# Moving the seventh product of a seven-product matrix multiply into the phase that makes its operands

## The chip, the cores and the metric

The kernel runs on one NeuronCore of a Trainium2 chip. The metric is the device time of one execution in microseconds (us). TensorE is called PE here, VectorE DVE, ScalarE ACT, GpSimd POOL, and SyncE, which only issues DMAs in this kernel, SP.

## The reference

Two stages are chained. The first is an attention between 512 tokens and 32 state vectors for 8 batches and 8 heads of width 64, in both directions. The second is a feed-forward layer on its 8 x (512 + 32) = 4352 output rows of width 512.

```python
scores = 0.125 * x @ state^T;  xread = softmax(scores) @ state        # 512 rows per batch
scores2 = 0.125 * state @ x^T; sread = softmax(scores2) @ x           # 32 rows per batch
y = concat([xread, sread], rows)                                      # [4352, 512]
h = y @ w_in;  g = h * sigmoid(h);  out = g @ w_out                   # 512 -> 2048 -> 512
```

The max that the reference takes off before each exp is left out by the kernel; the softmax is the same without it.

## The kernel before, in words

Everything is issued in an order written out by hand; no scheduler reorders it. Each engine, and each DMA queue, works through its own list in that order and stops at an instruction whose inputs or buffers aren't ready.

For one batch the hidden layer is made transposed, in 16 tiles of 128 hidden units by 512 tokens. One such tile is a "G1 step" (`emit_G1`): two matmuls with 512 columns each on the normalised attention weights `aT` and on `W1` (the state times `w_in`, made by small matmuls `ps_w1` and copied to SBUF in "pieces" of 512 columns, one half by DVE and the other by ACT), and one ACT instruction that applies silu and writes `g`. `upto(k)` issues all G1 steps up to number k. The tiles of `h` go through two PSUM banks (`h1`), used in turn.

The output product g @ w_out (G2) is done for the first batch, number 0, and for the 256 gathered sread rows, numbered as batch 8, with plain matmuls. For batches b = 1 to 7 class `Unit` does it by Strassen's scheme in Winograd's form: tokens are halved (columns 0:256 and 256:512 of `g`), hidden units are halved (`lo` = tiles 0 to 7, `hi` = tiles 8 to 15), output columns are halved, and seven half-size products take the place of eight. Product p has 8 "unit steps" (`u.mm(p, k)`), each two matmuls with 256 columns. Right sides are the quarters of `w_out` (B11 to B22) and their sums D1 to D4 (`wt`). Left sides are quarters of `g` and sums `s1`, `s2` and others that DVE forms (`sums12`, `sums3`, `sums4`). Products 2, 3 and 4 go to a PSUM bank `be`, the others are added up in a bank `al`; the two banks are tags `o0` and `o1` and change places from batch to batch. In between, copies of `al` are taken (`snap`), and the four blocks of the output tile pair `o[0]`, `o[1]` (`block(i, c)`) are put together by adds on DVE and POOL. `out_half(i)` stores one tile.

One batch b runs like this on PE. (1) The G1 phase: the remaining G1 steps of the batch (6 are already done for b > 1), with 13 unit steps of products 1 and 2 strewn in (`early`). (2) The rest of product 2, and "group A" (`group_a`): `ps_w1` pieces, transposed scores of a later batch, and for some batches the `ps_sr` matmuls. For b = 1 scores of batch 2 come before product 6, and group A after it. (3) Products 6, 4, 5. (4) "Group B": up to three more `ps_w1` pieces, for b = 1, 2, 3, 4 and 6; where there are three, the third goes through the `h1` banks. (5) Products 3 and 7 with the first six G1 steps of the next batch (or steps of batch 8 at b = 7) between them. What is left of a batch, the last copy, add and store (`finish_last`), is issued in the next batch's G1 phase.

Beside this run: the x tiles of later batches, fetched by SP DMAs (`fetch_x`), cast by POOL (`cast_x`, four casts), transposed by SP DMA transposes (`transpose_x`); the attention's normalisation (`norm`, `norm_t`; the latter's multiplication is shared by POOL and DVE) and the DMA transpose of its result to `aT`; copies of x rows (`spread_x`), of states (`evict_state`), and the rest of the weight sums (`t_weights`) on DVE in the first G1 phases. ACT changes its function table to exp and back to silu once per batch up to b = 5: after product 2 for `exps_t`, and back after the `snap` that follows product 6; the copies of group A's `W1` pieces stand behind that.

Of the kernel before, what the change touches and what calls it, by code (L numbers as in the profile page):

```python
# [8 lines left out]
FP32 = mybir.dt.float32  # L9
# [9 lines left out]
B = 8  # L19
# [6 lines left out]
NFT = DF // 128  # L26
# [16 lines left out]
def kernel(  # L43
# [8 lines left out]
    nc = tc.nc  # L52
    ds = bass.ds
# [104 lines left out]
    def copy(eng, dst, src):  # L158
        if eng is nc.scalar:
            nc.scalar.activation(dst, src, func=COPY, bias=0.0)  # L160
        else:
            eng.tensor_copy(dst, src)  # L162
# [407 lines left out]
    def G2(b, tt, ft):  # L570
        if ft == 0:
            if b == 0 and tt >= 2:
                outs[tt] = psA.tile([128, DM], FP32, tag=f"a{tt - 2}", name="o_a")
            else:
                i = tt % 2
                outs[tt] = psO.tile([128, DM], FP32, tag=f"o{i}", name="o")
        nc.tensor.matmul(  # L577
            outs[tt][:],
            gt[b * NFT + ft][:, ds(128 * tt, 128)],
            w_out_sb[:, ft, :],  # L580
            start=(ft == 0),
            stop=(ft == NFT - 1),
            skip_group_check=True,
        )
# [5 lines left out]
    def sub(eng, dst, a, c):  # L590
        eng.tensor_tensor(dst, a, c, op=SUB)  # L591

    def add(eng, dst, a, c):
        eng.tensor_tensor(dst, a, c, op=ADD)  # L594
# [13 lines left out]
    class Unit:  # L608
        def __init__(self, b):
            self.b = b  # L610
            self.lo, self.hi = gh[b, 0], None
            self.s1 = spool.tile([128, 8, 256], BF16, tag="s1", name="s1")
            self.s2 = spool.tile([128, 8, 256], BF16, tag="s2", name="s2")
            self.al = psO.tile([128, 2, 256], FP32, tag=f"o{b % 2}", name="o")
            self.be = None
            self.o = [
                opool.tile([128, 2, DM], FP32, tag=f"o_sb{i}", name="o_sb") for i in range(2)
            ]

        def snap(self, eng):  # L620
            t = spool.tile([128, 2, 256], FP32, tag=f"snap{len(self.kept) % 2}", name="snap")
            self.kept.append(t)
            copy(eng, t[:], self.al[:])

        kept = None

        def mm(self, p, k):
            hi, lo = self.hi, self.lo
            left, right = {
                1: (lambda: lo[:, k, 0:256], B11),  # L630
                2: (lambda: hi[:, k, 0:256], B21),
                3: (lambda: hi[:, k, 0:256], B22),
                4: (lambda: hi[:, k, 256:512], D4),
                5: (lambda: self.s1[:, k], D1),
                6: (lambda: self.s2[:, k], D2),
                7: (lambda: lo[:, k, 256:512], D3),
            }[p]
            left = left()
            if p in (2, 3, 4):
                if k == 0:  # L640
                    self.be = psO.tile(
                        [128, 2, 256], FP32, tag=f"o{1 - self.b % 2}", name="o"
                    )
                to, first = self.be, k == 0
            else:
                to, first = self.al, p == 1 and k == 0
            for t in range(2):
                nc.tensor.matmul(  # L648
                    to[:, t, :],
                    left[:, ds(128 * t, 128)],  # L650
                    right[:, k, :],
                    start=first and t == 0,
                    stop=(k == 7),
                    skip_group_check=True,
                )
# [11 lines left out]
        def sums3(self):  # L667
            for k0 in (0, 4):
                k = ds(k0, 4)
                sub(nc.vector, self.lo[:, k, 256:512], self.lo[:, k, 0:256], self.lo[:, k, 256:512])  # L670

        def block(self, i, c):
            return self.o[i][:, :, ds(256 * c, 256)]
# [179 lines left out]
    PIECES_B = {1: 3, 2: 3, 3: 3, 4: 3, 6: 2}  # L853
    LEADS = 6

    def finish_last(u):
        copy(nc.scalar, u.block(1, 1), u.al[:])
        add(nc.gpsimd, u.block(1, 0), u.block(1, 0), u.block(1, 1))
        u.out_half(1)
# [6 lines left out]
    prev = None  # L866
    for b in range(1, B):
        n = b + 1
        m = n + 1
        u = Unit(b)  # L870
        u.kept = []
        lead = 3 if b == 1 else LEADS
        todo = [(1, k) for k in range(8)] + [(2, k) for k in range(8)]
        n_todo = len(todo)

        def early(j):
            while (
                todo
                and (8 * (todo[0][0] - 1) + todo[0][1]) <= j - 2
                and (n_todo - len(todo)) * (NFT - lead) < 13 * (j + 1 - lead)  # L880
            ):
                u.mm(*todo.pop(0))
                if len(todo) == 8:
                    u.snap(nc.vector)

        for j in range(lead, NFT):
            upto(NFT * b + j + 1)
            if j == 8:
                u.hi = gh[b, 1]
            if j == lead + 1:  # L890
                if prev is not None:
                    finish_last(prev)
                if b == 1:
                    transpose_x(3)
                    t_weights((2, 4, 3), 4, 4)
# [12 lines left out]
                if 1 < b and m + 1 < B:  # L908
                    fetch_x(m + 1)
            early(j)  # L910
            if j == 13:
                u.sums12(0, 4)
        srs = SREAD_AT.get(b, ())

        def group_a():
# [3 lines left out]
            ps_sr = sread(srs, bank if m < B else new_h) if srs else None  # L919
            return pss, ps_sr  # L920

        u.sums12(4, 2)
        while todo:
            if len(todo) == 2 and 1 < b < B - 1:
                made = group_a()
            u.mm(*todo.pop(0))
        u.sums12(6, 2)
        add(nc.vector, u.block(0, 0), u.be[:], u.kept[0][:])
        if b == 1:
            for hg in range(2):  # L930
                scores(2, hg)
# [10 lines left out]
        def sread_g1(step):  # L942
            if n == B:
                upto(NFT * B + (step + 1) * NFT // 34)

        step = 0
        for k in range(8):
            u.mm(6, k)
            if n == B and k > 5:
                sread_g1(step)  # L950
                step += 1
        u.snap(nc.scalar)
        if b == 1:
            for hg in range(2):
                norm(2, hg)
# [2 lines left out]
            exps_t(m)  # L958
            fetch_x(m + 1)
        if b > 1:  # L960
            u.sums4()
        if n < B:
            if m < B:
                nc.scalar.activation(warm[:], busy[:, 0:1], func=SILU, bias=0.0)
# [3 lines left out]
            for piece in made[0][1:]:  # L968
                w1_out(*piece)
        if b == 1:  # L970
            u.sums4()
        for k in range(8):
            u.mm(4, k)
            sread_g1(step)
            step += 1
        add(nc.vector, u.block(1, 0), u.be[:], u.kept[1][:])
        if 1 < b and m + 1 < B:
            transpose_x(m + 1)
        u.sums3()
        for k in range(8):  # L980
            u.mm(5, k)
            sread_g1(step)
            step += 1
        u.snap(nc.scalar)
# [6 lines left out]
        for p in (3, 7):  # L991
            for k in range(8):
                u.mm(p, k)
                sread_g1(step)
                step += 1
                i = 8 * (p == 7) + k
                if n < B and i % 2 == 1 and 0 < i // 2 <= LEADS:
                    upto(NFT * n + i // 2)
            if b == 1 and p == 3:
                for c in range(4):  # L1000
                    cast_x(m + 1, nc.gpsimd, c, 1)
                transpose_x(m + 1)
            if p == 3:
                add(nc.vector, u.block(0, 1), u.be[:], u.kept[2][:])
                u.out_half(0)
        prev = u
        for ft in range(NFT):
            gt.pop(NFT * b + ft)
    finish_last(prev)
    for ft in range(NFT):  # L1010
        upto(NFT * B + ft + 2)
        G2(B, 0, ft)
# [32 lines left out]
```

## Time and profile before

| | |
|---|---|
| median of 3 runs | 203.4 us (203.1 to 205.5) |
| profiled execution, its own time | 203.08 us |
| its span, first to last instruction | 201.3 us |
| PE busy | 195.3 us (97%) |
| ACT busy | 141.0 us (70%) |
| DVE busy | 126.9 us (63%) |
| POOL busy | 60.8 us (30%) |
| granted PE clock | full in every slice |
| DMA traffic | 28.71 MB, mean 143 GB/s |

The span is what the profile sees; the 1.8 us between it and the execution's own time lie before its first and after its last instruction. Busy PE time counts pipelined matmuls with modelled ends, so the distance between the starts of successive matmuls says more than their durations. From 38 us on, the time is a row of seven batches of some 21 us, and from 190.6 us a tail with batch 8's output product.

### The profile page before, as it was taken

The page shows a single profiled execution, that of the slowest core. Times are in us where ns is not written, and L with a number is a line of the kernel's source. Part 1 is how long each engine was busy: PE and PEld are TensorE (multiplying, and loading weights), DVE is VectorE, ACT ScalarE, POOL GpSimd, SP SyncE. Part 2 cuts the span into 40 slices and gives each one's busy share as a digit, 9 for nine tenths or more (in the row PEclk, how much of TensorE's full clock was granted, in tenths as well). Part 3 has the DMA queues.
Part 4 walks back from the last instruction along what each step waited for, and adds up shares of the span by engine and source line. Part 5 has one row for each costly group of instructions (what it writes and reads, how often), then busy time and mean ns, then how long its engine had stood idle before and what let it go on. Part 6 is the DMA issues. An engine that isn't in the chain of part 4 may idle for free.

```text
span 201.3 us, 4661 instructions
## 1 busy us (share of the span) xinstructions
PE 195.3 (97%) x1912; PEld 129.6 (64%) x1912; DVE 126.9 (63%) x244; ACT 141.0 (70%) x251; POOL 60.8 (30%) x79
## 2 busy tenths in 40 slices
PE   7799999999999999999999999999999999999992
PEld 2444445456866586668666776668666766688862
DVE  3862756999988797558864798187617972832101
ACT  2875667899787897789868777897784478545420
POOL 8674343730425504240804071400140022002020
PEclk9999999999999999999999999999999999999999
DMA  5999999994282797759164947142214020200222
GB/s 185 193 202 206 242 266 346 247 239 96 35 220 80 234 261 138 208 160 242 45 182 135 253 50 215 45 118 55 104 44 116 7 87 27 104 3 0 104 111 101
DMA packets 40965, 28.71 MB, mean 143 GB/s; under 512 B 27376, under 2 KB 37616, under 8 KB 40944
## 3 DMA queue, kind: packets, MB, share of 16 engines
q1 hardware_dynamic: 34736, 20.65, 38.4%
q0 software_dynamic: 5920, 7.64, 18.4%
q8 instruction: 15, 0.25, 0.5%
q10 hardware_dynamic: 288, 0.13, 0.3%
q14 instruction: 6, 0.05, 0.1%
HBM read 17.43 MB, written 8.91 MB: 131 GB/s over the span
## 4 chain that ended last, share of the span: by engine, by line
PE 94%; DMA 2%; DVE 1%; ACT 1%; issue 0%
PE o L648 43%; PE h L540 27%; PE o L577 5%; PE ps_w L473 5%; PE h L558 3%; PE o_a L577 3%; DMA x_f<-in_x_dram 2%; PE o_part L698 2%; PE ps_xt L257 1%; PE ps_sr L420 1%; PE ps_sc L310 1%; ACT xT L160 1%; PE ps_busy L168 1%; PE ps_scT L336 1%; PE ps_at L402 1%; PE h L522 0%
## 5 line engine op out<-in xcount | busy, mean ns | idle before, releaser
L568 ACT ACTIVATE g<-h 128x512 bf16<-128x512 f32 (+1 forms) x142 | 80.1, 575 | 29.0 <-PE h L540 20.1
L648 PEld LDWEIGHTS <-g 128*128 128x128 bf16 x560 | 53.7, 98 | 33.2 <-issue 3.1
L540 PE MATMUL h<-aT,W 128*128 128x512 bf16 x252 | 73.8, 379 | 0.1
L648 PE MATMUL o<-w_out_sb,g 128*128 128x256 bf16 x336 | 53.5, 273 | 0.1
L648 PE MATMUL o<-wt,g 128*128 128x256 bf16 x224 | 30.8, 273 | 0.0
L540 PEld LDWEIGHTS <-W 128*128 128x128 bf16 x252 | 24.4, 98 | 7.6 <-issue 0.7
L162 POOL CAST x_nat<-x_f 128x512 bf16<-128x512 f32 x24 | 17.4, 764 | 34.0 <-DMA x_f<-in_x_dram 28.3
L648 PE MATMUL o<-wt,s 128*128 128x256 bf16 x224 | 27.4, 273 | 0.0
L594 DVE TENSOR_TENSOR o_sb<-o,snap 128x512 f32<-128x512 f32 x21 | 14.5, 689 | 18.7 <-PE o L648 15.5
L162 DVE CAST W<-ps_w 128x512 bf16<-128x512 f32 (+1 forms) x35 | 21.8, 665 | 6.4 <-PE ps_w L473 6.4
L648 PEld LDWEIGHTS <-s 128*128 128x128 bf16 x224 | 21.9, 98 | 2.5
L591 POOL TENSOR_TENSOR o_sb<-o_sb,snap 128x512 f32<-128x512 f32 x7 | 8.9, 1269 | 37.3 <-ACT snap L160 37.3
L594 POOL TENSOR_TENSOR o_sb<-o_sb 128x512 f32<-128x512 f32 x7 | 8.9, 1266 | 36.7 <-ACT o_sb L160 36.7
L162 DVE COPY snap<-o 128x512 f32<-128x512 f32 x7 | 4.8, 691 | 23.3 <-PE o L648 19.1
L160 ACT ACTIVATE W<-ps_w 128x512 bf16<-128x512 f32 (+1 forms) x31 | 16.2, 580 | 2.8 <-PE ps_w L473 2.8
L160 ACT ACTIVATE snap<-o 128x512 f32<-128x512 f32 x14 | 8.4, 597 | 14.0 <-PE o L648 9.7
L577 PE MATMUL o<-w_out_sb,g 128*128 128x512 bf16 x48 | 13.2, 380 | 0.0
L577 PEld LDWEIGHTS <-g 128*128 128x128 bf16 x80 | 7.3, 98 | 8.7 <-issue 0.8
L594 DVE TENSOR_TENSOR s<-g 128x512 bf16<-128x512 bf16 (+1 forms) x21 | 11.5, 549 | 1.7 <-ACT g L568 1.6
L591 DVE TENSOR_TENSOR s<-s,g 128x512 bf16<-128x512 bf16 (+1 forms) x21 | 10.8, 514 | 0.7
L473 PE MATMUL ps_w<-w_in_sb,stT 64*32 64x512 bf16 (+1 forms) x264 | 10.2, 375 | 0.0
L591 DVE TENSOR_TENSOR g<-g 128x1024 bf16<-128x1024 bf16 x14 | 10.1, 759 | 0.0
(93 smaller groups left out, 191.6 us busy)
## 6 DMA issues: line engine op xcount, KB each, us to landing
out_dram<-o_sb SPq DMA_DIRECT2D x14, 512.0 KB, 2.8
x_f<-in_x_dram SPq DMA_DIRECT2D x6, 512.0 KB, 5.3
x_f<-in_x_dram POOLq DMA_DIRECT2D x2, 1024.0 KB, 11.6
x_f<-in_x_dram SPq DMA_DIRECT2D x2, 1024.0 KB, 6.5
w_out_sb<-in_moe_w_out_dram POOLq DMA_DIRECT2D x6, 256.0 KB, 11.3
w_in_sb<-in_moe_w_in_dram POOLq DMA_DIRECT2D x3, 512.0 KB, 10.6
out_dram<-o_sb SPq DMA_DIRECT2D x5, 256.0 KB, 5.7
x_f<-in_x_dram POOLq DMA_DIRECT2D x2, 512.0 KB, 14.6
```

Of the source, the lines that this page charges most:

```text
L160: nc.scalar.activation(dst, src, func=COPY, bias=0.0)
L162: eng.tensor_copy(dst, src)
L168: nc.tensor.matmul(ps[:], busy[:, 0:128], busy[:], start=True, stop=True, skip_group_check=True)
L473: nc.tensor.matmul(pss[f, hg][ds(32 * s, 32), 0:n], stT[ds(r, 64), b, h // 2, s % 2, :], w_in_sb[ds(r, 64), h // 2, ds(f, n)], start=True, ...
L540: nc.tensor.matmul(h_ps[k][:], W1[b][:, hg, ds(128 * ft, 128)], aT[b][:, hg, :, :], start=(hg == 0), stop=(hg == 1), skip_group_check=True,)
L558: nc.tensor.matmul(ps[:, 0:256], w_in_sb[:, kt, ds(128 * ft, 128)], xmT[:, :, kt].rearrange("p t n b -> p t (n b)"), start=(kt == 0), stop ...
L568: nc.scalar.activation(gt[k], ps[:, 0:n], func=SILU, bias=0.0)
L577: nc.tensor.matmul(outs[tt][:], gt[b * NFT + ft][:, ds(128 * tt, 128)], w_out_sb[:, ft, :], start=(ft == 0), stop=(ft == NFT - 1), skip_gr ...
L591: eng.tensor_tensor(dst, a, c, op=SUB)
L594: eng.tensor_tensor(dst, a, c, op=ADD)
L648: nc.tensor.matmul(to[:, t, :], left[:, ds(128 * t, 128)], right[:, k, :], start=first and t == 0, stop=(k == 7), skip_group_check=True,)
L698: nc.tensor.matmul(ps[:, 0:n], gt[b * NFT + ft][:, ds(128 * tt, 128)], w_out_sb[:, ft, cols], start=(ft == 0), stop=(ft == NFT - 1), skip_ ...
```

## The change

Product 7 changes places with product 2: it is formed in the G1 phase, together with product 1, since it needs `lo` only. Its left side, a difference of two token halves of `lo`, is therefore formed in the G1 phase too (`sums3`, in two pieces, at j = 6, or 4 for b = 1, and at j = 9). Products 7, 2, 4 and 3 use the bank `be`, which is now always `o0`; 1, 6 and 5 add up in `al`, always `o1`. There are no separate `snap` tiles: `keep` copies `al` straight into a block of the output tiles, and later adds work on that block in place. `s2` is formed straight from `hi` and the new difference, one instruction per piece where it was two; `s1` is formed from `s2` later, behind product 6's issue. The add after product 6 on POOL comes right after its copy on ACT. Group B comes before product 5, not after it; the first two G1 steps of the next batch come in product 5, the other four in product 3, the last product. `finish_last` is gone; both stores are issued in the batch itself.

```diff
@@ G2: the bank of batch 8's first output tile
-                i = tt % 2
+                i = 1 if b == B else tt % 2
@@ class Unit
-            self.al = psO.tile([128, 2, 256], FP32, tag=f"o{b % 2}", name="o")
+            self.al = psO.tile([128, 2, 256], FP32, tag="o1", name="o")
...
-        def snap(self, eng):
-            t = spool.tile([128, 2, 256], FP32, tag=f"snap{len(self.kept) % 2}", name="snap")
-            self.kept.append(t)
-            copy(eng, t[:], self.al[:])
+        def keep(self, eng, i, c):
+            copy(eng, self.block(i, c), self.al[:])
...
-            if p in (2, 3, 4):
+            if p in (7, 2, 4, 3):
                 if k == 0:
-                    self.be = psO.tile([128, 2, 256], FP32, tag=f"o{1 - self.b % 2}", name="o")
+                    self.be = psO.tile([128, 2, 256], FP32, tag="o0", name="o")
...
-        def sums12(self, k0, n):
-            add(nc.vector, self.s1[:, k], self.lo[:, k, 256:512], self.hi[:, k, 256:512])
-            sub(nc.vector, self.s2[:, k], self.s1[:, k], self.lo[:, k, 0:256])
+        def sums3(self, k0, n):
+            sub(nc.vector, self.lo[:, k, 256:512], self.lo[:, k, 0:256], self.lo[:, k, 256:512])
+        def sums2(self, k0, n):
+            sub(nc.vector, self.s2[:, k], self.hi[:, k, 256:512], self.lo[:, k, 256:512])
+        def sums1(self):
+            for k0 in (0, 4):
+                add(nc.vector, self.s1[:, k], self.s2[:, k], self.lo[:, k, 0:256])
@@ the G1 phase of batch b
-        todo = [(1, k) for k in range(8)] + [(2, k) for k in range(8)]
+        todo = [(p, k) for p in (1, 7) for k in range(8)]
...
-                and (8 * (todo[0][0] - 1) + todo[0][1]) <= j - 2
-                and (n_todo - len(todo)) * (NFT - lead) < 13 * (j + 1 - lead)
+                and todo[0][1] + (0 if todo[0][0] == 1 else 2) <= j - 2
+                and (n_todo - len(todo)) * (NFT - lead) < 16 * (j + 1 - lead)
             ):
                 u.mm(*todo.pop(0))
                 if len(todo) == 8:
-                    u.snap(nc.vector)
+                    u.keep(nc.vector, 0, 0)
...
             if j == lead + 1:
-                if prev is not None:
-                    finish_last(prev)
                 if b == 1:
                     transpose_x(3)
-                    t_weights((2, 4, 3), 4, 4)
+                    t_weights((3, 2, 4), 4, 4)
...
+            if j == max(lead, 4):
+                u.sums3(0, 4)
+            if j == 9:
+                u.sums3(4, 4)
             early(j)
             if j == 13:
-                u.sums12(0, 4)
+                u.sums2(0, 4)
@@ after the G1 phase
-        u.sums12(4, 2)
         while todo:
-            if len(todo) == 2 and 1 < b < B - 1:
-                made = group_a()
             u.mm(*todo.pop(0))
-        u.sums12(6, 2)
-        add(nc.vector, u.block(0, 0), u.be[:], u.kept[0][:])
+        copy(nc.vector, u.block(1, 1), u.be[:])
+        u.sums2(4, 2)
+        if 1 < b < B - 1:
+            made = group_a()
+        u.sums2(6, 2)
+        for k in range(8):
+            u.mm(2, k)
+        add(nc.vector, u.block(0, 0), u.block(0, 0), u.be[:])
...
-        (product 6) ; u.snap(nc.scalar)
+        units(6)
+        u.keep(nc.scalar, 1, 0)
+        add(nc.gpsimd, u.block(1, 0), u.block(1, 0), u.block(1, 1))
...
-            u.sums4()
+            u.sums1()
...
-        (product 4) ; add(nc.vector, u.block(1, 0), u.be[:], u.kept[1][:])
+        units(4)
+        add(nc.vector, u.block(1, 0), u.block(1, 0), u.be[:])
...
-        u.sums3()
-        (product 5) ; u.snap(nc.scalar)
-        sub(nc.gpsimd, u.block(1, 0), u.block(1, 0), u.kept[2][:])
+        u.sums4()
         (group B)
-        (products 3 and 7, with G1 steps 1 to 6 of the next batch)
-        (after product 3:) add(nc.vector, u.block(0, 1), u.be[:], u.kept[2][:]); u.out_half(0)
+        units(5, {5: 1, 7: 2})
+        u.keep(nc.scalar, 0, 1)
+        add(nc.gpsimd, u.block(1, 1), u.block(1, 1), u.block(0, 1))
+        u.out_half(1)
+        units(3, {1: 3, 3: 4, 5: 5, 7: 6})
...
+        add(nc.vector, u.block(0, 1), u.block(0, 1), u.be[:])
+        u.out_half(0)
```

Lines in round brackets stand for loops that are shortened here. `units(p, leads)` issues the 8 steps of product p and the next batch's G1 steps at the places that `leads` names; for b = 7 it spreads the 16 G1 steps of batch 8 over 26 unit steps (34 before).

More of the change, by code (lines that the diff above doesn't have):

```diff
@@ L618, in __init__ @@
             ]
-        def snap(self, eng):
-            t = spool.tile([128, 2, 256], FP32, tag=f"snap{len(self.kept) % 2}", name="snap")
-            self.kept.append(t)
-            copy(eng, t[:], self.al[:])
-        kept = None
+        def keep(self, eng, i, c):
+            copy(eng, self.block(i, c), self.al[:])
         def mm(self, p, k):
@@ L638, in mm @@
             left = left()
-            if p in (2, 3, 4):
+            if p in (7, 2, 4, 3):
                 if k == 0:
-                    self.be = psO.tile(
-                        [128, 2, 256], FP32, tag=f"o{1 - self.b % 2}", name="o"
-                    )
+                    self.be = psO.tile([128, 2, 256], FP32, tag="o0", name="o")
                 to, first = self.be, k == 0
@@ L655, in mm @@
                 )
-        def sums12(self, k0, n):
+        def sums3(self, k0, n):
             k = ds(k0, n)
-            add(nc.vector, self.s1[:, k], self.lo[:, k, 256:512], self.hi[:, k, 256:512])
-            sub(nc.vector, self.s2[:, k], self.s1[:, k], self.lo[:, k, 0:256])
+            sub(nc.vector, self.lo[:, k, 256:512], self.lo[:, k, 0:256], self.lo[:, k, 256:512])
+        def sums2(self, k0, n):
+            k = ds(k0, n)
+            sub(nc.vector, self.s2[:, k], self.hi[:, k, 256:512], self.lo[:, k, 256:512])
+        def sums1(self):
+            for k0 in (0, 4):
+                k = ds(k0, 4)
+                add(nc.vector, self.s1[:, k], self.s2[:, k], self.lo[:, k, 0:256])
         def sums4(self):
@@ L665, in sums4 @@
                 sub(nc.vector, self.hi[:, k, 0:256], self.hi[:, k, 0:256], self.s2[:, k])
[L667 to L670, printed above, removed]
         def block(self, i, c):
@@ L854 @@
     LEADS = 6
[L856 to L859, printed above, removed]
     def fetch_x(i):
@@ L864, in fetch_x @@
             load_x(i, h, n, nc.sync)
-    prev = None
     for b in range(1, B):
@@ L870 @@
         u = Unit(b)
-        u.kept = []
         lead = 3 if b == 1 else LEADS
-        todo = [(1, k) for k in range(8)] + [(2, k) for k in range(8)]
+        todo = [(p, k) for p in (1, 7) for k in range(8)]
         n_todo = len(todo)
@@ L941, with units @@
                 cast_x(m + 1, nc.gpsimd, c, 1)
-        def sread_g1(step):
-            if n == B:
-                upto(NFT * B + (step + 1) * NFT // 34)
         step = 0
[L947 to L952, printed above, removed]
+        def units(p, leads={}):
+            nonlocal step
+            for k in range(8):
+                u.mm(p, k)
+                if n == B and (p != 6 or k > 5):
+                    upto(NFT * B + (step + 1) * NFT // 26)
+                    step += 1
+                if n < B and k in leads:
+                    upto(NFT * n + leads[k])
+        units(6)
+        u.keep(nc.scalar, 1, 0)
+        add(nc.gpsimd, u.block(1, 0), u.block(1, 0), u.block(1, 1))
         if b == 1:
@@ L970 @@
         if b == 1:
[L971 to L976, printed above, removed]
+            u.sums1()
+        units(4)
+        add(nc.vector, u.block(1, 0), u.block(1, 0), u.be[:])
         if 1 < b and m + 1 < B:
             transpose_x(m + 1)
-        u.sums3()
[L980 to L984, printed above, removed]
-        sub(nc.gpsimd, u.block(1, 0), u.block(1, 0), u.kept[2][:])
+        u.sums4()
         if b in PIECES_B:
@@ L990 @@
                 w1_out(*pss[i])
[L991 to L1006, printed above, removed]
+        units(5, {5: 1, 7: 2})
[3 more added lines that the diff above has]
+        units(3, {1: 3, 3: 4, 5: 5, 7: 6})
+        if b == 1:
+            for c in range(4):
+                cast_x(m + 1, nc.gpsimd, c, 1)
+            transpose_x(m + 1)
+        add(nc.vector, u.block(0, 1), u.block(0, 1), u.be[:])
+        u.out_half(0)
         for ft in range(NFT):
             gt.pop(NFT * b + ft)
-    finish_last(prev)
     for ft in range(NFT):
```

## The prediction

> **What bounds the kernel now.** I read the page first: engine shares, then the chain that ended last.
>
> ```profile
> span 201.3 us, 4661 instructions
> PE 195.3 (97%) x1912; PEld 129.6 (64%) x1912; DVE 126.9 (63%) x244; ACT 141.0 (70%) x251; POOL 60.8 (30%) x79
> PE 94%; DMA 2%; DVE 1%; ACT 1%; issue 0%
> ```
>
> PE holds 94% of the chain. To see whether it runs at its pace or only looks busy, I took the timeline of the batch b = 3 and compared starts.
>
> ```profile
> 82.80 0.59 PE L540 MATMUL h<-aT,W 128*128 128x512 bf16 x2
> ...
> 91.57 1.91 PE L648 MATMUL o<-wt,s 128*128 128x256 bf16 x16
> 93.32 1.91 PE L648 MATMUL o<-wt,g 128*128 128x256 bf16 x16
> 95.06 1.91 PE L648 MATMUL o<-wt,s 128*128 128x256 bf16 x16
> 96.90 0.84 PE L473 MATMUL ps_w<-w_in_sb,stT 64*32 64x512 bf16 x24
> 97.68 1.05 PE L648 MATMUL o<-w_out_sb,g 128*128 128x256 bf16 x8
> 98.56 0.59 PE L540 MATMUL h<-aT,W 128*128 128x512 bf16 x2
> 98.99 0.60 PE L648 MATMUL o<-w_out_sb,g 128*128 128x256 bf16 x4
> ```
>
> A product starts every 1.75 us (91.57, 93.32, 95.06), so a unit step takes 0.218; a G1 step takes 0.43 (98.56 to 98.99). One batch holds 56 unit steps (12.2), 16 G1 steps (6.9) and the small matmuls of groups A and B (0.77 and 0.78): 20.7 us. It lasts 20.97 (G1 step j = 6 starts at 82.80 and, in the next batch, at 103.77). So PE loses 0.3 us per batch, 2 us in seven. Whatever the change does to the other engines, it can't gain more than that, since it takes no matmul off PE. The question is which new waits PE gets.
>
> [...]
>
> **The change, part by part.** Work: DVE forms `s1`, `s2` with 5 instructions for 6, but copies two accumulators per batch for one; ACT drops one 0.6 us copy per batch. None of this is on the chain; PE covers it. DMA bytes are the same. What counts are places in the queues. These rows hold the prices:
>
> ```profile
> 44.32 0.69 DVE L162 COPY x_rows<-x_nat 128x2048 bf16<-128x2048 bf16 x1
> 50.40 2.05 POOL L386 TENSOR_TENSOR an<-exp_nat,rc 128x512 bf16<-128x512 bf16 x2 [8.39 <-DVE rc L384]
> 78.48 2.28 POOL L162 CAST x_nat<-x_f 128x512 bf16<-128x512 f32 x4 [10.34 <-DMA x_f<-in_x_dram]
> 91.77 0.69 DVE L594 TENSOR_TENSOR o_sb<-o,snap 128x512 f32<-128x512 f32 x1 [0.24 <-PE o L648]
> 93.52 0.60 ACT L160 ACTIVATE snap<-o 128x512 f32<-128x512 f32 x1 [0.41 <-PE o L648]
> 94.13 1.28 ACT L964 ACT_TABLE_LOAD   x1
> 95.54 1.06 ACT L160 ACTIVATE W<-ps_w 128x512 bf16<-128x512 f32 x2
> 95.73 3.20 POOL L162 CAST x_nat<-x_f 128x512 bf16<-128x512 f32 x4 [7.94 <-DMA x_f<-in_x_dram]
> 98.89 1.27 POOL L591 TENSOR_TENSOR o_sb<-o_sb,snap 128x512 f32<-128x512 f32 x1
> ```
>
> 1. *Product 7's bank.* Product 2 now starts in the bank that product 7 has just filled, so PE waits for DVE's copy of it; before, products 2 and 4 were a whole product apart. The trace has no such wait. DVE starts 0.2 to 0.37 after the end of a product (91.57 to 91.77; 95.06 to 95.43), takes 0.69, and PE starts some 0.1 after a DVE copy (`W` done 98.45, G1 at 98.56): 1.0 to 1.2, I take 1.05. For b = 2, 3, 5 group A (0.77) stands between and leaves 0.28; for b = 4 and 6 it is longer, with its `ps_sr` matmuls, and hides it. For b = 1 and 7 nothing does.
>
> 2. *The first difference at b = 1.* Product 7's first step falls in G1 step j = 9, at 43.06 (42.19 for j = 9 before, plus one unit step more at j = 3, plus 0.43 and 0.22). Its difference stands on DVE behind weight sums, state copies and the x copy that ends at 45.01; with 0.65 of its own, PE starts at 45.7. Wait: 2.6. Everything of b = 1 comes later by that.
>
> 3. *The add on POOL at b = 1.* It waits for ACT's copy after product 6, and the two `an` multiplications stand behind it. Product 7 ends at 50.0 (45.7 + 0.22 + six G1 steps and seven unit steps), product 2 starts at 51.05, scores take 0.47, product 6 ends at 55.0, ACT's copy at 55.8, the add at 57.1 (1.26), `an` at 58.15 and 59.2 (before: 51.4, 52.45). SP issues the first `aT` transpose at 58.2 and the second, as before, 2.5 later at 60.7; it lands 2.4 (least) to 3.2 (median) after issue, 63.1. PE reaches the first G1 step of batch 2 at 57.04 without stalls (61.82, less 3.48 for product 3 with four G1 steps, 0.43 + 0.44 + 0.43 for the rest of product 5), with items 1 and 2 at 60.7. Wait: 2.4. So b = 1 costs 2.6 + 1.05 + 2.4 = 6.05.
>
> 4. *Group B ahead of product 5.* Its pieces take the banks of group A, which ACT clears late: copy after product 6 (+0.2, 0.6), table load 1.28, warm 0.1, then two copies of 0.53, done 2.75 and 3.3 after product 6's end. With product 5 in front, PE came at 3.5 (93.32 to 96.90); now it comes at 1.75, waits until 2.85 and 3.4, and is through at 3.95 rather than 2.6: 1.35 for b = 3. For b = 4 only the second pair of banks waits for ACT: 2.85 less 2.05, 0.8. For b = 6 DVE is last (add 0.9, two sums 1.28, copy, four reciprocals, the multiplication, copy: 4.5 after product 2, so 2.8 after product 6): 0.9.
>
> [...]
>
> 5. *DVE behind POOL.* DVE's add after product 4 needs POOL's add, and that now stands behind the four casts, which wait for x from HBM. Behind DVE's add stand the two `sums4` (1.28) and the copy of the piece in an `h1` bank (0.65), which frees the bank of the second G1 step of the next batch, now in product 5. Before, POOL's op only had to reach the store. In b = 3, counted from step j = 6: `aT` no longer waits for the last batch's final POOL add, but DVE's own add and the first difference come first, so SP issues the fetch at 5.65 (6.35 before); casts start 6.6 later (89.15 to 95.73), at 12.2, end at 15.4; POOL's add 16.7, DVE's 17.4, sums 18.7, copy 19.4, PE 19.5. PE would be there at 20.97 - 3.91 + 0.28 + 1.35 = 18.7: 0.8. For b = 4, by the same steps: 1.0 (19.7 against 18.65). An x landing takes 4.1 to 6.6, so each is 0 to 1.
>
> 6. *b = 2.* Its fetch stands on SP behind everything from the `aT` transposes of item 3, which come 6.7 late; one store of 0.6 no longer stands between. Casts start at 78.48 + 6.1, say 84.6, end at 86.9; POOL's add takes 1.26, DVE's 0.69, sums 1.28, copy 0.65, and 0.1 lies at each of three handovers: PE's second G1 step of batch 3 at 91.05. Its place without stalls is 82.80 - 3.91 = 78.9, so b = 1 and 2 together cost 12.1. Smaller waits of b = 2 (state copies ahead of the second difference 1.3; items 1 and 4) lie inside that; they are 2.9 if the casts come early.
>
> The last store and add of a batch, now inside it, are hidden behind the next G1 phase (`keep` on DVE waits for the store's landing, 2.8 after issue; it is due some 4 us on).
>
> Sum: 12.1 (b = 1, 2) + 2.4 (b = 3: 0.28 + 1.35 + 0.8) + 1.8 (b = 4) + 0.3 (b = 5) + 0.9 (b = 6) + 1.05 (b = 7) = 18.6. The span becomes 219.9; with the 1.8 us around it, 221.7, against the profiled 203.08 (0.3 below the median). A measurement of this kernel can tell about 2% from no change; this is 9%.
>
> **Rivals.** *Bank waits only.* If x lands early and the `aT` transposes overlap, items 3, 5 and 6 vanish. Left: 2.6, item 1 with 1.05 x 2 + 0.28 x 3 = 2.95, item 4 with 1.35 x 2 + 0.8 + 0.9 = 4.4, and 1.3 at b = 2: 11.2, so 214.3. For it: POOL is busy 30% only. Against it: its casts wait for x in every batch (10.34, 7.94).
>
> *Late x everywhere.* If b = 3 and b = 4 keep b = 2's delay, because POOL's and SP's lists never catch up, each loses some 3 us more: 227.6. Against it: from b = 3 on SP has nothing ahead of the fetch but `aT`.
>
> *Not slower by 2%.* The G1 phase gets 16 unit steps for 13 and so 0.65 us more PE work under which DVE and ACT can run ahead. If that lead carries through, group B finds its banks clear and only item 1 stays: 203.08 + 2.95 = 206.0. It decides from the point where ACT's copies of group A end 1.1 us earlier after product 6 than now; against it, they wait for product 6 itself, not for a lead.
>
> **How the numbers follow.** Forecast 221.7 at 0.67; bank waits only 0.19; late x 0.09; not slower 0.05. The range 212 to 228 takes in the first three and their landing bounds and leaves the last out. Faster by over 2% would need more than the 2 us that PE loses: 0.01. Within 2%: 0.04. Slower: 0.95.
>
> **What would show it.** In the profile after: a PE gap of 2.6 before product 7 of b = 1, gaps of about 1 before product 2 at b = 1 and 7, gaps ahead of the `ps_w` groups ended by ACT's `W` copies, and gaps ahead of the first two G1 steps ended by `aT` (b = 1) and by DVE (b = 2). PE's busy time unchanged, its share down to near 89%. Wrong, if batches last under 21.5 us, or if no gap follows POOL's casts.

## The result, and the profile after

The changed kernel takes 217.25 us (median of 4 runs, 217.0 to 217.8) against 203.4: ratio 1.066, 95% interval [1.059, 1.074]. The forecast was 221.7 with a range of 212 to 228. The sign, the range and the kind of cost (PE waits in a batch that had none) were right; the sum was 4.4 too high, and it was made up differently. The measured time lies nearer to the rival "bank waits only" (214.3) than to the forecast.

The page of the changed kernel: span, busy shares, the granted TensorE clock in 40 slices, the chain that ended last.

```profile
span 215.7 us, 4637 instructions
PE 198.4 (92%) x1893; PEld 130.4 (60%) x1912; DVE 133.7 (62%) x244; ACT 137.4 (64%) x244; POOL 62.4 (29%) x79
PEclk9999999979999999999999999999999999999999
PE 71%; DVE 12%; ACT 6%; issue 5%; DMA 3%; POOL 1%; POOLq 0%; DVEq 0%
```

PE's share of the chain fell from 94% to 71%. The one digit 7 in the clock row (slice 9, 43 to 48 us) has no counterpart before and is taken up below.

PE's timeline, where it waits: start, duration, operation, and in brackets the idle time ahead and what ended it.

```profile
45.52 0.61 PE L642 MATMUL o<-wt,g 128*128 128x256 bf16 x2 [2.52 <-DVE g L591]
...
52.44 1.80 PE L642 MATMUL o<-w_out_sb,g 128*128 128x256 bf16 x15 [0.78 <-DVE o_sb L162]
...
63.41 0.38 PE L540 MATMUL h<-aT,W 128*128 128x512 bf16 x1 [0.83 <-DMA aT<-an]
...
77.02 0.39 PE L642 MATMUL o<-wt,g 128*128 128x256 bf16 x2 [2.82 <-DVE g L591]
...
105.73 1.91 PE L642 MATMUL o<-wt,g 128*128 128x256 bf16 x16
107.57 0.39 PE L473 MATMUL ps_w<-w_in_sb,stT 64*32 64x512 bf16 x1
108.63 1.11 PE L473 MATMUL ps_w<-w_in_sb,stT 64*32 64x512 bf16 x23 [0.67 <-ACT W L160]
109.67 1.49 PE L642 MATMUL o<-wt,s 128*128 128x256 bf16 x12
...
189.28 1.91 PE L642 MATMUL o<-w_out_sb,g 128*128 128x256 bf16 x16 [0.78 <-DVE o_sb L162]
```

In order: the first difference at b = 1, the bank copy ahead of product 2, the second `aT` transpose, the second difference at b = 2, group B at b = 3 (the rows at 86.13 and 131.85 are alike for b = 2 and 4), the bank copy at b = 7. Product 4 to product 5 at b = 3 takes 3.94 (105.73 to 109.67) where a product and the same group took 2.62 before (95.06 to 97.68 in the rows of the prediction): the loss is 1.3, not the 0.67 in the bracket, since the group issued one matmul early and then stood still.

The same on the engines that PE waits for: DVE at b = 1 and b = 2, then ACT, POOL and DVE around product 6 of b = 2.

```profile
42.35 1.78 DVE L162 COPY stT<-st_x 64x64 bf16<-64x64 bf16 x8
44.16 0.69 DVE L162 COPY x_rows<-x_nat 128x2048 bf16<-128x2048 bf16 x1
44.77 1.29 DVE L591 TENSOR_TENSOR g<-g 128x1024 bf16<-128x1024 bf16 x2
...
69.01 3.53 DVE L162 COPY stT<-st_x 64x128 bf16<-64x128 bf16 x8
...
74.82 1.53 DVE L162 COPY x_rows<-x_nat 128x2048 bf16<-128x2048 bf16 x1
76.28 0.68 DVE L591 TENSOR_TENSOR g<-g 128x1024 bf16<-128x1024 bf16 x1
77.09 0.69 DVE L162 COPY o_sb<-o 128x512 f32<-128x512 f32 x1
...
83.49 0.60 ACT L160 ACTIVATE o_sb<-o 128x512 f32<-128x512 f32 x1 [1.66 <-issue]
84.10 1.28 ACT L964 ACT_TABLE_LOAD   x1
85.39 0.20 ACT L964 ACTIVATE warm<-busy 128x1 f32<-128x1 bf16 x1
85.50 1.06 ACT L160 ACTIVATE W<-ps_w 128x512 bf16<-128x512 f32 x2
...
83.46 2.28 POOL L162 CAST x_nat<-x_f 128x512 bf16<-128x512 f32 x4 [7.65 <-DMA x_f<-in_x_dram]
85.70 1.27 POOL L594 TENSOR_TENSOR o_sb<-o_sb 128x512 f32<-128x512 f32 x1
87.00 0.69 DVE L594 TENSOR_TENSOR o_sb<-o_sb,o 128x512 f32<-128x512 f32 x1 [2.22 <-POOL o_sb L594]
```

The difference that PE waits for ends at 76.96, behind state copies of 3.53 and an x copy of 1.53. ACT's copies of group A's pieces come behind the table load, as item 4 says (84.10, 85.50). DVE idles 2.22 us for POOL's add, which stands behind the casts, as items 5 and 6 say; yet PE loses next to nothing there (0.18 ahead of the second G1 step of batch 3, at 89.55).

The cost by batch, with every kernel that was run. A batch lasts from the silu of G1 step j = 6 to the same point of the next; the last column runs from there at b = 7 to the end. Each star is 3.4 us at half the granted clock inside that batch.

| kernel | median, ratio [95%] | b=1 | 2 | 3 | 4 | 5 | 6 | rest |
|---|---|---|---|---|---|---|---|---|
| before | 203.3 | 21.58 | 20.98 | 20.98 | 21.75 | 20.10 | 21.17 | 33.89 |
| after | 217.25, 1.066 [1.059, 1.074] | 27.80* | 25.49 | 22.34 | 22.88 | 20.11 | 21.74 | 34.46 |
| b_late | 217.36, 1.071 [1.064, 1.077] | 27.74 | 26.13* | 21.88 | 22.77 | 20.11 | 21.08 | 34.45 |
| casts_late | 218.72, 1.076 [1.070, 1.083] | 27.74* | 26.64* | 22.32 | 22.72 | 20.11 | 21.74 | 34.47 |
| evict_early | 218.06, 1.074 [1.070, 1.078] | 26.03 | 27.22* | 22.34 | 22.87 | 20.11 | 21.74 | 34.45 |
| evict_casts | 218.15, 1.073 [1.068, 1.077] | 27.69* | 26.84* | 22.32 | 22.72 | 20.11 | 21.74 | 34.45 |
| evict_store | 217.28, 1.068 [1.065, 1.072] | 27.81* | 24.58 | 22.33 | 22.97 | 20.11 | 21.74 | 34.48 |
| b2_free | 215.37, 1.059 [1.056, 1.063] | 29.56** | 22.69 | 22.31 | 22.72 | 20.11 | 21.74 | 34.45 |
| sum_first | 213.55, 1.052 [1.048, 1.055] | 23.45 | 26.81* | 22.34 | 22.94 | 20.11 | 21.74 | 34.44 |
| own_bank | 215.81, 1.062 [1.058, 1.067] | 26.68* | 26.82* | 22.34 | 22.97 | 20.11 | 21.74 | 33.52 |
| before_b_early | 207.74, 1.023 [1.019, 1.026] | 21.89 | 22.25 | 22.25 | 22.54 | 20.10 | 21.83 | 33.87 |
| all_b_early | 208.02, 1.027 [1.020, 1.033] | 21.75 | 22.86 | 22.32 | 22.73 | 20.11 | 21.74 | 33.53 |
| all_leads | 208.47, 1.026 [1.023, 1.028] | 23.28 | 21.99 | 21.99 | 22.88 | 20.40 | 21.38 | 33.57 |
| all_b_mid | 206.16, 1.014 [1.012, 1.016] | 21.95 | 22.04 | 21.79 | 22.58 | 20.11 | 21.09 | 33.53 |

The kernel before was measured again beside each group of runs (medians 203.2 to 203.4), and each ratio is against its own. The batch columns come from one profiled execution each. Executions of one kernel spread by 0.6 to 3.1 us, as much as many of these edits are worth, so the columns, read with their stars, are the sharper view of a single edit.

### The profile page after: what moved, and what is told of

Read it like the earlier page. It is cut to its first block, busy times and chain, and to the rows that moved or that the text cites. A ratio compares the mean times of both kernels' runs of the same rounds, so it can differ in the third digit from the quotient of the medians.

```text
span 215.7 us, 4637 instructions
## 1 busy us (share of the span) xinstructions
PE 198.4 (92%) x1893; PEld 130.4 (60%) x1912; DVE 133.7 (62%) x244; ACT 137.4 (64%) x244; POOL 62.4 (29%) x79
## 4 chain that ended last, share of the span: by engine, by line
PE 71%; DVE 12%; ACT 6%; issue 5%; DMA 3%; POOL 1%; POOLq 0%; DVEq 0%
PE o L642 30%; PE h L540 21%; PE o L577 5%; PE ps_w L473 3%; PE h L558 3%; PE o_a L577 3%; DVE stT L162 2%; DMA x_f<-in_x_dram 2%; DVE W L162 2%; ACT L964 2%; PE o_part L695 2%; ACT eT L350 1%; DVE wt L591 1%; DVE o_sb L162 1%; POOL an L386 1%
## 5 line engine op out<-in xcount | busy, mean ns | idle before, releaser
L540 PE MATMUL h<-aT,W 128*128 128x512 bf16 x237 | 70.8, 384 | 0.9 <-DMA aT<-an 0.8
L642 PE MATMUL o<-w_out_sb,g 128*128 128x256 bf16 x336 | 48.7, 273 | 1.9 <-DVE o_sb L162 1.6
L594 POOL TENSOR_TENSOR o_sb<-o_sb 128x512 f32<-128x512 f32 x14 | 17.7, 1265 | 82.3 <-ACT o_sb L160 82.3
L594 DVE TENSOR_TENSOR o_sb<-o_sb,o 128x512 f32<-128x512 f32 x21 | 14.4, 687 | 42.8 <-PE o L642 37.8
L642 PE MATMUL o<-wt,g 128*128 128x256 bf16 x224 | 33.2, 278 | 5.4 <-DVE g L591 5.3
L160 ACT ACTIVATE o_sb<-o 128x512 f32<-128x512 f32 x16 | 9.5, 595 | 17.1 <-issue 7.5
L162 DVE COPY o_sb<-o 128x512 f32<-128x512 f32 x15 | 10.3, 686 | 10.3 <-PE o L642 10.2
L366 POOL TENSOR_TENSOR an<-e,rcn 128x512 bf16<-128x512 bf16 x5 | 7.8, 1552 | 16.2 <-DVE rcn L364 16.2
L594 DVE TENSOR_TENSOR s<-s,g 128x1024 bf16<-128x1024 bf16 x14 | 10.9, 820 | 0.0
L577 PE MATMUL o_a<-w_out_sb,g 128*128 128x512 bf16 x31 | 9.8, 379 | 0.2
```

The source lines that it names most:

```text
L366: eng.tensor_tensor(a[:, hg], e2[b][:, hg], rc[:, hg].to_broadcast([128, 4, 4, NS]), op=MULT)
L540: nc.tensor.matmul(h_ps[k][:], W1[b][:, hg, ds(128 * ft, 128)], aT[b][:, hg, :, :], start=(hg == 0), stop=(hg == 1), skip_group_check=True,)
L577: nc.tensor.matmul(outs[tt][:], gt[b * NFT + ft][:, ds(128 * tt, 128)], w_out_sb[:, ft, :], start=(ft == 0), stop=(ft == NFT - 1), skip_gr ...
L642: nc.tensor.matmul(to[:, t, :], left[:, ds(128 * t, 128)], right[:, k, :], start=first and t == 0, stop=(k == 7), skip_group_check=True,)
```

## The experiments

My theory after the result: the prediction's waits are real, but several fall due at the same moment, so they don't add. The rival: the waits add, and their sizes were simply smaller. They differ most at b = 2, which is where most of the first runs look.

**b_late, casts_late: items 4 and 5 undone, one at a time.**

```diff
 b_late
-        (group B)
         units(5, {5: 1, 7: 2})
+        (group B)
 casts_late
-        if 1 < b and m + 1 < B: (four casts on POOL)      # ahead of product 6
         add(nc.gpsimd, u.block(1, 0), u.block(1, 0), u.block(1, 1))
+        if 1 < b and m + 1 < B: (four casts on POOL)
```

> Group B goes back behind product 5, all else as in the changed kernel. In its trace PE loses 1.26 us (b = 2), 1.26 (b = 3), 0.8 (b = 4), 0.6 (b = 6) and 0.25 (b = 1) at the bank waits of group B. If waits add up, the time falls by 4.2 us, to 213.0. If a wait that is taken away only uncovers the next one (aT at b = 1; sums4 and the W copy, behind POOL's add, at b = 2 and 3), it falls by 2.6, to 214.6. If ACT's late copies are not the cause, it stays at 217.

> POOL's add after product 6 is issued ahead of the four casts (b = 2, 3, 4), all else as in the changed kernel. By items 5 and 6 of the prediction this chain sets the end of three batches, and the time should fall by some 3 us, to 214. By the trace of the changed kernel, where the second G1 step of the next batch waits 0.18 us at b = 2 and nothing at b = 3 and 4, it falls by 0.2 at most: 217.0 to 217.3.

Neither moved the total. b_late won 0.46, 0.11 and 0.66 at b = 3, 4 and 6, and 1.1 at b = 2 once its half-clock stretch (1.7) is taken off: 2.3 where item 4 had 4.4. It gave 1.6 of that back at b = 1, which held a half-clock stretch in after and none here and still lasts as long: without group B in front, product 5 comes before DVE has its left side `s1`, PE then waits for `aT` as in after, and group B, which stood ahead of that wait, now comes behind it. PE's timeline of b_late at b = 1:

```profile
58.38 1.05 PE L642 MATMUL o<-wt,s 128*128 128x256 bf16 x8 [0.30 <-DVE s L594]
59.83 0.61 PE L642 MATMUL o<-wt,s 128*128 128x256 bf16 x4 [0.41 <-DVE s L594]
...
61.62 0.38 PE L540 MATMUL h<-aT,W 128*128 128x512 bf16 x1 [0.96 <-DMA aT<-an]
...
62.79 0.41 PE L473 MATMUL ps_w<-w_in_sb,stT 64*32 64x512 bf16 x8
```

casts_late changed b = 3 by 0.02 and b = 4 by 0.16 where item 5 had 0.8 and 1.0: that item is nothing. Its b = 2 is longer by its half-clock stretch: 3.41 us of it, 0.65 of them idle, cost an estimated 1.4 (half of the rest), and 26.64 less 1.4 is 25.2.

**evict_early, evict_casts: the wait of b = 2.** The state copies that stand ahead of the second difference go to the end of b = 1; in evict_casts with POOL's add ahead of the casts too.

```diff
                 elif n < B:
-                    if b == 2: (evict_state(v, nc.vector, 4, 4) for both v)
@@ ahead of product 5
+        if b == 1: (evict_state(v, nc.vector, 4, 4) for both v)
```

> The eight state copies that DVE does in the G1 phase of b = 2 are issued at the end of b = 1, in front of product 5, where DVE then idles 2.6 us; all else as in the changed kernel. The 2.8 us wait of product 7 at b = 2 should go. If waits add up: 2.8 less, 214.4. If the chain of x fetch, casts, POOL add, DVE add stands right behind it, the second G1 step of batch 3 moves only with SP's aT transpose, some 1.3 earlier: 216.0.

> Both of the two edits before: state copies early, and POOL's add ahead of the casts. If the cast chain was hidden behind the wait for the state copies, the two together give more than each by itself summed: 3.0 less than the changed kernel, 214.2, where the two alone give 1.3 and 0.2. If waits simply add up, this equals the state copies alone less 0.2.

The gap of 2.82 shrank to 0.26, and a gap of the same size opened one product later. evict_early's PE, DVE and SP timelines at b = 2 (SP's rows are its DMA issues):

```profile
73.58 0.39 PE L642 MATMUL o<-wt,g 128*128 128x256 bf16 x2 [0.26 <-DVE g L591]
...
79.12 1.22 PE L642 MATMUL o<-w_out_sb,g 128*128 128x256 bf16 x5 [2.76 <-DVE o_sb L162]
...
77.18 0.69 DVE L162 COPY o_sb<-o 128x512 f32<-128x512 f32 x1 [3.66 <-DMA out_dram<-o_sb]
...
78.39 0.68 DVE L162 COPY o_sb<-o 128x512 f32<-128x512 f32 x1
...
71.56 1.65 SPq L147 DMA_TRANSPOSE xT<-x_nat  x1
73.30 0.54 SPq L673 DMA_DIRECT2D out_dram<-o_sb  x1
```

DVE's `keep` after product 1 (77.18) writes the output block that the last store of b = 1 must have read; the copy of product 7's bank, for which product 2 waits, stands behind it on DVE (78.39). SP issues this store behind the x transpose, which waits for POOL's casts, and it lands 3.8 after issue. In after, the store landed at 77.00 and the difference ended at 76.96: the two waits ended together, so taking away the first alone gained nothing (the store alone wasn't tried). evict_casts shows the same: its gap, 2.41 us, opens at the same copy. This is the sentence of the prediction that called the last store hidden; at b = 2 it isn't.

**evict_store, b2_free: both waits, then the third.** evict_store adds to evict_early that SP issues the store ahead of the x transpose; b2_free adds casts_late as well.

```diff
             for c in range(4):
                 cast_x(m + 1, nc.gpsimd, c, 1)
-            transpose_x(m + 1)
         add(nc.vector, u.block(0, 1), u.block(0, 1), u.be[:])
         u.out_half(0)
+        if b == 1: transpose_x(m + 1)
```

> Two waits stand side by side at b = 2: DVE's second difference behind the state copies, and DVE's copy after product 7 behind the landing of the last store of b = 1, which SP issues behind the x transpose that waits for POOL's casts. Taking away the first alone moved no time. Here both are taken away: the state copies stand at the end of b = 1, and the store is issued ahead of the x transpose. If these two waits are what b = 2 costs, its 25.49 us become 22.5 to 22.9, and the total 213.4 to 214.6 (2.8 less, and up to 1.0 less again if the slow clock after the gap goes too). If a third thing is due at the same time (the casts and POOL's add, as item 6 of the prediction has it), b = 2 stays at 25 and the total at 217.

> The two edits that free the state copies and the store of b = 1, and with them POOL's add ahead of the casts (b = 2, 3, 4). With the first two alone batch 2 lasted 24.58 us and lost 1.69 at the second G1 step of batch 3, behind POOL's casts, as item 6 of the prediction has it; with the last alone it lost nothing less than before. If these three are all that b = 2 waits for besides group B, batch 2 goes to 22.4 to 23.0, there is no gap over 0.7 in it and no slow clock, and the total is 215.0 to 215.6. If there is a fourth wait of that size, batch 2 stays above 24.

With both gone, a third one appears, and it is item 6. evict_store's PE, POOL and DVE timelines:

```profile
89.40 0.59 PE L540 MATMUL h<-aT,W 128*128 128x512 bf16 x2 [1.69 <-DVE W L162]
...
83.32 2.28 POOL L162 CAST x_nat<-x_f 128x512 bf16<-128x512 f32 x4 [8.73 <-DMA x_f<-in_x_dram]
85.56 1.26 POOL L594 TENSOR_TENSOR o_sb<-o_sb 128x512 f32<-128x512 f32 x1
86.86 0.69 DVE L594 TENSOR_TENSOR o_sb<-o_sb,o 128x512 f32<-128x512 f32 x1 [3.90 <-POOL o_sb L594]
```

Casts, POOL's add, DVE's add, sums, `W` copy, second G1 step: the chain of item 6, link by link, 1.69 us late once PE comes earlier. b2_free takes it out: batch 2 falls to 22.69, and only group B's wait (0.67 in its bracket) and one of 0.21 are left. So batch 2's 4.5 us are three waits side by side (2.8), group B (1.3) and some 0.4 of small ones. The median gained 1.9 rather than 2.8; the profiled execution shows a longer first gap (3.10) and two half-clock stretches at b = 1.

**sum_first, own_bank: b = 1 and item 1.**

```diff
 sum_first
-                    t_weights((3, 2, 4), 4, 4)
-                    (evict_state, spread_x(2))
+                    t_weights((3,), 4, 4)
+                    u.sums3(0, 4)
+                    t_weights((2, 4), 4, 4)
 (and at j = 9, behind the second difference: evict_state, spread_x(2))
 own_bank
+                    if p == 7 and self.b in (1, 7): self.be = bank([128, 2, 256], FP32, "o")
```

> The first difference of b = 1 goes to the front of DVE's list; the weight sums 2 and 4, the state copies and the x copy follow it. If the gap of 2.5 us ahead of product 7 and the slow clock behind it (some 1 us) are a cost of their own, batch 1 goes from 27.80 to about 24.3 and the total to 213.8, or 214.8 if the clock drops at another gap instead. If another wait of the same length stands behind it in b = 1 (the aT transposes, then 0.83, would grow), batch 1 stays above 26.5 and the total above 216.

> At b = 1 and b = 7 product 7 gets a PSUM bank of its own, so that product 2 needn't wait for DVE's copy. Prediction's item 1 (1.05 each, measured gaps 0.78 each plus the start of the next product): 217.25 - 1.8 = 215.4. If b = 1 gives its share back to the next wait (the aT transposes), only b = 7 is won: 216.4, with batch 1 unchanged at 27.8 and the last stretch at 33.6.

Here things add. sum_first took 4.35 us off batch 1, the gap of 2.52 and the half-clock stretch behind it (1.7), and the `aT` wait stayed at 0.82. own_bank took 1.12 off batch 1 (0.20 of it because its first gap was 2.32 rather than 2.52) and 0.94 off the last stretch, which is then 0.37 shorter than before.

**before_b_early: item 4 by itself, in the kernel before.**

```diff
+        (group B)
         (product 5) ; u.snap(nc.scalar) ; sub(nc.gpsimd, ...)
-        (group B)
```

> The kernel before with one edit: group B is issued ahead of product 5 rather than behind it. Prediction's item 4 by itself, with no other wait beside it: 1.3 each at b = 2, 3, 4, 0.9 at b = 6, and up to 1.3 at b = 1: 203.2 + 4.8 to 6.1 = 208.0 to 209.3. If the wait is smaller where nothing else of the change is there (ACT one step further ahead), 205 to 206; if PE has slack for it, 203.5.

Costs of 0.31, 1.27, 1.27, 0.79, 0 and 0.66 for b = 1 to 6: 4.3 in sum. The prediction had 1.35 (b = 2, 3), 0.8 and 0.9, and nothing for b = 1. PE's timeline at b = 3:

```profile
95.24 1.91 PE L648 MATMUL o<-wt,g 128*128 128x256 bf16 x16
97.08 0.39 PE L473 MATMUL ps_w<-w_in_sb,stT 64*32 64x512 bf16 x1
98.08 1.11 PE L473 MATMUL ps_w<-w_in_sb,stT 64*32 64x512 bf16 x23 [0.62 <-ACT W L160]
99.13 1.92 PE L648 MATMUL o<-wt,s 128*128 128x256 bf16 x16
```

**all_b_early, all_leads, all_b_mid: everything else taken away.** all_b_early joins b2_free, sum_first and own_bank, and at b = 1 puts POOL's two `an` multiplications ahead of its add. The other two move group B in it.

```diff
 all_leads
-        (group B)
-        units(5, {5: 1, 7: 2})
+        units(5)
+        (group B)
-        units(3, {1: 3, 3: 4, 5: 5, 7: 6})
+        units(3, {2: 1, 3: 2, 4: 3, 5: 4, 6: 5, 7: 6})
 all_b_mid (in units)
                 u.mm(p, k)
+                if p == 5 and k == 2 and b in PIECES_B: (group B)
```

> All waits taken away except group B's place, which stays ahead of product 5: b2_free's three edits, the first difference of b = 1 first, product 7's own bank at b = 1 and 7, and POOL's attention weights ahead of its add at b = 1. If the waits found so far are the whole loss, what is left is item 4 of the prediction, 4.4 as the kernel before showed it by itself: 203.3 + 4.4 = 207.7, less 0.4 that the own bank won below the time of before at b = 7: 207.3. If masked waits remain, 210 or more.

> As all_b_early, and group B stands behind product 5 again with all six G1 steps of the next batch behind it, in product 3 (two of them stood in product 5). If ACT's copies are the only thing that group B waited for, nothing of the loss stays: 203.0 to 204.0, the same as before. If the six G1 steps now wait for the banks that ACT and DVE clear behind the third piece, some 0.5 stays in each of four batches: 205 to 206. Faster than before by more than 1 us is excluded by PE's own pace.

> As all_b_early, with group B inside product 5, behind three of its eight unit steps. Ahead of group B PE then comes 0.65 us later, so that 0.6 of the 1.26 us wait for ACT's copies stays at b = 2, 3, 4 and nothing of the 0.47 at b = 6; behind it three unit steps (0.65) are left to cover the copies of the third piece, whose banks the next G1 step takes, which costs 0.1 to 0.2. If the two sides add up so, 208.0 - 1.4 to 2.0 = 206.0 to 206.6. If what is won ahead of group B is lost behind it one for one, as all_leads suggests, 207.7 to 208.2.

all_b_early came to 208.0, where the kernel before with group B's move alone came to 207.7. No half-clock stretch is left in its batches. all_leads lost at other places what it won: PE's and DVE's timelines of it at b = 1 and b = 2:

```profile
60.39 0.59 PE L540 MATMUL h<-aT,W 128*128 128x512 bf16 x2 [1.02 <-DVE W L162]
...
83.03 0.59 PE L540 MATMUL h<-aT,W 128*128 128x512 bf16 x2 [0.50 <-ACT g L568]
...
57.39 2.23 DVE L162 COPY stT<-st_x 64x128 bf16<-64x128 bf16 x8
59.65 1.89 DVE L162 CAST W<-ps_w 128x512 bf16<-128x512 f32 x3
```

The row at 83.03 is the rival that its expectation named: six G1 steps in a row of eight unit steps wait for the silus that clear their banks. It is half of what this kernel loses at b = 2 (1.01); the rest isn't accounted for. The one at 60.39 is a fault of this kernel: my edit left the state copies ahead of group B's copies on DVE at b = 1. all_b_mid shares the cover between the two sides of group B, and won 1.9 as worked out. PE's timeline at b = 3:

```profile
99.53 1.51 PE L473 MATMUL ps_w<-w_in_sb,stT 64*32 64x512 bf16 x24
100.98 0.83 PE L645 MATMUL o<-wt,s 128*128 128x256 bf16 x6
101.78 0.38 PE L540 MATMUL h<-aT,W 128*128 128x512 bf16 x1
```

Group B takes 1.45 from start to start rather than 0.78, and 0.15 is lost after it. This is the best version with the moved product, and at 206.16 it is still 1.4% slower than before. What keeps it there is about 0.8 to 1.1 us in each of b = 2, 3 and 4. That the eight unit steps of product 7, which the kernel before had behind group B as cover for the next batch's G1 steps, are what is missing, fits all three placings of group B; it wasn't tried apart from them.

## Why the prediction was right or wrong

- *PE has no slack, so every new wait is paid.* Right where a wait is the last to end, and the base of the whole; of waits that end together only one is paid. The span grew by 14.4 us, from 201.3 to 215.7.
- *Item 2*, 2.6: measured 2.52. Right. What it left out is the clock: after the gap the granted clock was 0.50 for 3.41 us. evict_early and evict_casts have the same first batch, one without this stretch and one with: 26.03 and 27.69, so it costs 1.7, half of 3.41.
- *Item 1*: 0.92 to 0.94 where 1.05 was priced. For b = 2, 3, 5 group A covered nearly all of the 0.28 (batch 5 is 0.01 longer).
- *Item 3*, 2.4: measured 0.83. The landing was right (63.36, forecast 63.1), because the two transposes followed each other by 1.46 rather than 2.5 but began later; PE arrived at 62.6 rather than 60.7, held up by the half clock that wasn't forecast. So b = 1 came out at 6.2 for 6.05 with one term missing and another too large: that it agrees is luck.
- *Item 4*: the size was right when measured by itself (before_b_early: 4.3 for 4.4, 0.31 of it at b = 1). In after it is paid in full too, 1.3 at b = 3, with 0.65 to 0.67 in the brackets. Undoing it in b_late returned 2.3 and lost 1.6 of that at b = 1. At b = 2 of b_late, group B behind a product 5 with two G1 steps takes 1.09 from start to start rather than 0.78 (88.92 to 90.01), and the next G1 step then waits for ACT's copies (0.19 in its bracket, at 90.82); at b = 1 the group only changed sides with the `aT` wait (62.79, behind it).
- *Item 5*, 1.8: nothing. The step that failed is the length of the chain at b = 3. Counted from step j = 6, at 93.45, the casts began at 11.8 (forecast 12.2) and took 2.79 us (3.2), and DVE's copy was done at 18.4 (19.4); PE's second G1 step came at 18.4 too (111.88; forecast 18.7), held until then by group B, and waited for nothing. This is the first part of the error of 4.4.
- *Item 6*: the chain is real, but it ran 1.1 to 1.5 us earlier than forecast (casts at 83.46 and the G1 step at 89.55, forecast 84.6 and 91.05), and so it was no later than two other waits. One of those I had priced at 1.3, taking the state copies at their earlier length: they took 3.53 and the x copy 1.53, and the gap was 2.82. The other, the store, I had called hidden. Batch 2 cost 4.5 for 6.05, the second part of the error. The rest lies in batches 5, 6 and the last stretch: 0.01, 0.57 and 0.57 for 0.3, 0.9 and 1.05.
- *Rivals.* "Bank waits only" gave 214.3 and came nearer than the forecast. With the state copies at their measured length and 1.7 for the clock it would have been 217.5, partly by luck: it has 2.95 for item 1, which cost some 1.9, and nothing for the `aT` wait of 0.83. "Late x everywhere" fell with item 5, "not slower by 2%" with the sign.
- *What would show it.* The gaps of b = 1 and 7 and of group B stand in PE's timeline above. The prediction's own sign of being wrong, no gap behind POOL's casts, came true (0.18 at b = 2): in the changed kernel items 5 and 6 weren't what PE paid for.
- *PE share near 89%*: it was 92%. The span is shorter than forecast, and PE's busy time, forecast unchanged, rose from 195.3 to 198.4. Half clock accounts for some 1.7 of that; where the rest comes from isn't shown (all_b_mid, without half clock in its batches, has 196.3).

## What to carry to other kernels

On in-order queues, waits that fall due at the same moment don't add, and removing one of them shows the next: here one edit to b = 2 gained nothing (its half-clock stretch taken off), two 0.9, three 2.8. Work out for each when it is due, take the latest, and list the runners-up; an experiment that removes one cause and changes nothing hasn't shown that cause to be false. A wait is best priced by its edit alone in a kernel that has no other wait: group B's place cost 4.3 us there, while undoing it amid the others moved the total by nothing.

## What the runs showed of the hardware

*Half clock followed long PE gaps here, but not every one.* In the changed kernel's profile the granted clock was full from 4.50 to 45.46 us, half for the next 3.41 us, and full from 48.87 to the end. Here are four stretches of that length, with PE busy time, instruction counts and the granted clock. The first holds the gap at b = 1, the second is the one at half clock; the gap at b = 2 falls into the last two.

```profile
core 0: us, PE busy (x) PEld busy (x) DVE busy (x) ACT busy (x) POOL busy (x), PEclk, DMA share, GB/s
42.05:45.46 3.41, 0.94 (x7) 0.40 (x5) 3.28 (x12) 1.25 (x3) 0.00 (x0) 1.00 1.26 239
45.46:48.87 3.41, 3.35 (x12) 1.80 (x13) 1.20 (x2) 1.17 (x2) 0.00 (x0) 0.50 0.39 87
72.76:76.18 3.42, 1.44 (x10) 0.66 (x7) 3.35 (x4) 1.53 (x3) 1.55 (x1) 1.00 0.98 277
76.18:79.59 3.41, 2.57 (x36) 1.43 (x36) 2.69 (x6) 1.43 (x3) 0.00 (x0) 1.00 0.73 184
```

In the first stretch PE idled 2.47 us, and the clock of the second was 0.50. The gap at b = 2 is longer, 2.82 for 2.52; PE idled 1.98 us of the third stretch and 0.84 of the fourth, and the clock stayed at 1.00. In evict_early the gap of 2.76 at b = 2 was followed by half clock (the row at 79.12: five matmuls in 1.22 us, where four take 0.60); the gap of 1.69 in evict_store wasn't (pairs of G1 matmuls in 0.59 at 89.40 as at 91.14). Nine kernels have stars in the table, 13 in all; the mean granted clock of their profiled executions was 0.982 to 0.992, that of the other five 0.996 to 1.000. What decides whether half clock follows a gap isn't shown; its length alone doesn't (2.52 and 2.76 were followed by it, 2.82 wasn't).

*DVE copies took longer beside POOL.* The x copy took 0.69 at 44.16, with POOL idle, and 1.53 at 74.82, while POOL multiplied (74.26 to 75.81); the eight state copies took 3.53 beside POOL's casts, and 2.23 in all_leads at 57.39, with POOL idle. The change itself brings this about: from b = 2 on its five x copies all meet POOL's multiplication and take 1.53 to 1.54, and the multiplication 1.55. In the kernel before they never meet: the copies take 0.68 or 0.69 (one, beside POOL's casts, 1.10), and the multiplication 1.04 or 1.05. What lengthens them isn't shown: no run here moved POOL away and left all else.
